# A long convolution and a mixture of experts on one core: eight batches in groups of 1, 2, 2, 2 and 1 in place of four groups of 2

## The chip, the core and the metric
The kernel runs on one core of a Trainium2 chip. The core has five engines with queues of their own: PE multiplies matrices and writes PSUM, DVE and ACT work on vectors in SBUF and PSUM, POOL (GpSimd) works on SBUF and issues the indirect transfers, SP issues nearly all others. The metric is the device time of one execution in microseconds (us), as a median of runs. Programs are compared on the same chip.

## The reference
There are 8 batches of 5696 tokens with 128 channels. First comes a causal convolution over the sequence with one filter `h` for each channel, done through a Fourier transform of twice the length. Its result is the input of a mixture of 8 experts: each token takes the one with the highest logit.
```python
y = irfft(rfft(x, n=2*S, axis=1) * rfft(h, n=2*S, axis=0)[None], n=2*S, axis=1)[:, :S]
x = y.reshape(B * S, D)                       # 45568 tokens of 128
logits = x @ w_gate + modality_bias[modality_id]
e_idx = argmax(logits, axis=1); probs = softmax(logits); gate_w = probs[range(N), e_idx]
for e in range(8):
    mask = e_idx == e
    out[mask] = gate_w[mask, None] * (maximum(x[mask] @ w1[e], 0) @ w2[e])   # 128 -> 1024 -> 128
```

## The kernel before
Most products are made from fp32 data split in two parts of a shorter type (`high`, `low`): ACT casts the high part, DVE or POOL subtracts it for the low part, and three matmuls stand for one.

The Fourier transform is split into stages, with results in DRAM between them. Stage 1 (`stage1`, for the first group `stage1_first`) transforms along 64 rows for each of 45 values of `q` and stores `z`. Stages 2 and 3 (`stage23`) go over 64 values of `k`: a matmul (`over`, L637), the product with the filter on DVE (L644), additions on POOL or DVE (L650, L651), the split of the sum into `yh` (ACT, L654) and `yl` (DVE or POOL, L657), the matmuls back (L663, or L667 to L669) and a store of `u`. Stage 4 (`stage4`) loads `u`, transforms back to tokens (L755, L756 or L761), turns them (L773), makes the logits (L780) and, by chunks of up to 4 pairs of `q`, routes: which expert, which place in the table `rows`, and an indirect store of 128 rows each by POOL (L880). A group is 2 batches; there are four, and they go through the stages one after the other, with the next group's earlier stages beside the later ones of this.

After some chunks (`CUTS`) the rows known so far are cut into a level of tiles of 512 rows of one expert; a table (`level`) says which expert and which rows. There are 7, 7, 22, 22 and 23 full tiles (0 to 80), and 23 tiles of 256 for what is left. A tile (`experts`) loads its rows (`mrt`, L962), turns them (L984), splits them, and goes through 8 steps of `gemm1` (L998 to L1000), `hh` (ACT, L1003), `hl` (DVE, L1006) and `gemm2` (L1014 to L1016); then it is turned back (L1023), scaled (L1026) and scattered to `out` by POOL (L1030). Weights are needed split. In the first two levels (`RAW`) each tile loads them raw in four halves and splits them (L973 to L980); meanwhile `split_weights` writes split weights of all experts to DRAM, and later levels load those (L969) where the expert changes.

The order on every engine is made when the program is built: `Plan.run` takes steps with given costs and due times (`AIMS`: knots for each stage, a lead for each kind of step) and lists them as they would start; a step that DVE or POOL (or ACT) may do goes to the one that is free. The engines then run their lists strictly in order. `BURST` and `SPACE` keep POOL's indirect transfers apart.

Of the kernel before, what the change touches and what calls it, by code (L numbers as in the profile page):

```python
# [1224 lines left out]
```

## Time and profile before
| what | us |
|---|---|
| median of 3 runs (2198.26 to 2200.70) | 2199.54 |
| the profiled execution | 2207.35 |
| its span, first to last instruction | 2205.6 |
| PE busy | 2049.7 |
| DVE busy | 1509.3 |
| ACT busy | 1190.1 |
| POOL busy | 1294.9 |

Busy times are of the whole span; the granted clock was 0.963 on average. Matmuls are pipelined, so that a busy PE may still run below its rate: how far apart matmuls start says more than how long one is recorded. A wait is put down to the instruction whose signal came last.

### The profile page before, as it was taken

The numbers are of one execution on the slowest core, as the hardware profiler recorded it, in microseconds if no ns is written. First come the engines' busy times: TensorE is split into PE (matmuls) and PEld (weight loads), VectorE is DVE, ScalarE is ACT, GpSimd is POOL, SyncE is SP. The second block draws the span as 40 slices with busy tenths as digits, with TensorE's granted clock in tenths as the row PEclk, the third lists the DMA queues.
The fourth block names the chain that finished last, engine by engine and source line by source line (L and its number), as shares of the span: only waits on it lengthen the run. The fifth ranks groups of instructions, "written<-read, shape, count | busy, mean of one in ns | idle before, by whom it ended". The sixth has DMA issues, their size and how long they took to land. (4 is left out here: it accounts for less than half of the span.)

```text
span 2205.6 us, 38243 instructions
## 1 busy us (share of the span) xinstructions
PE 2049.7 (93%) x11222; PEld 1677.4 (76%) x11222; DVE 1509.3 (68%) x2901; ACT 1190.1 (54%) x2415; POOL 1294.9 (59%) x1676
## 2 busy tenths in 40 slices
PE   5699989989999679999999999999999899999997
PEld 5577867767777567778887778888887688888997
DVE  5468936778557778977765899867677455555554
ACT  5645645445555456557764445566664344444443
POOL 2155726567577777745777777557777634334333
PEclk8889999999999989999999999999999999999999
DMA  8999899998998679965654656644341621214520
GB/s 276 312 297 319 278 280 319 309 281 270 315 307 252 200 216 287 280 210 161 202 182 146 199 156 185 204 157 125 120 150 58 148 68 44 84 42 159 191 75 21
DMA packets 236497, 434.77 MB, mean 197 GB/s; under 512 B 37317, under 2 KB 103849, under 8 KB 231680
## 3 DMA queue, kind: packets, MB, share of 16 engines
q1 hardware_dynamic: 212608, 384.17, 55.8%
q0 software_dynamic: 23680, 48.15, 6.7%
q8 instruction: 90, 1.47, 0.3%
q14 instruction: 119, 0.97, 0.1%
HBM read 408.13 MB, written 176.22 MB: 265 GB/s over the span
## 5 line engine op out<-in xcount | busy, mean ns | idle before, releaser
L1006 DVE SCALAR_TENSOR_TENSOR hl<-bank,hh 128x512 fp32r<-128x512 f32 x740 | 502.9, 686 | 264.2 <-ACT hh L1003 259.1
L1003 ACT ACTIVATE hh<-bank 128x512 fp32r<-128x512 f32 x740 | 440.1, 598 | 389.0 <-PE bank L1000 350.0
L1030 POOL DMA_INDIRECT out<-of,mrt x370 | 371.5, 1004 | 370.5 <-DVE of L1026 257.4
L880 POOL DMA_INDIRECT rows<-rt,idx x360 | 365.5, 1015 | 175.4 <-issue 102.3
L644 DVE TENSOR_TENSOR t<-bank,hs 96x512 f32<-96x512 f32 x420 | 266.9, 677 | 57.4 <-PE bank L637 29.7
L1014 PE MATMUL bank<-hh,slot 128*128 128x512 f32 (+1 forms) x736 | 304.1, 413 | 1.5 <-ACT hh L1003 1.2
L998 PE MATMUL bank<-mxh,slot 128*128 128x512 f32 (+1 forms) x736 | 302.6, 411 | 2.9 <-DVE hl L1006 1.0
L1015 PE MATMUL bank<-hl,slot 128*128 128x512 f32 (+1 forms) x736 | 283.2, 385 | 6.6 <-DVE hl L1006 6.6
L999 PE MATMUL bank<-mxl,slot 128*128 128x512 f32 (+1 forms) x736 | 284.6, 387 | 0.3
L1000 PE MATMUL bank<-mxh,slot 128*128 128x512 f32 (+1 forms) x736 | 283.9, 386 | 0.0
L1016 PE MATMUL bank<-hh,slot 128*128 128x512 f32 (+1 forms) x736 | 283.1, 385 | 0.0
L637 PE MATMUL bank<-zb,m 96*96 96x256 f32 x896 | 235.7, 391 | 12.6 <-DMA zb<-z 4.6
L637 PEld LDWEIGHTS bank<-zb,m 96*96 96x96 f32 x896 | 145.4, 167 | 61.5 <-DVE t L644 6.6
L654 ACT CAST yh<-t 96x512 fp32r<-96x512 f32 x142 | 87.4, 619 | 148.3 <-POOL t L651 60.0
L998 PEld LDWEIGHTS bank<-mxh,slot 128*128 128x128 f32 x736 | 141.6, 192 | 34.0 <-issue 3.0
L1000 PEld LDWEIGHTS bank<-mxh,slot 128*128 128x128 f32 x736 | 141.1, 192 | 29.5
L1016 PEld LDWEIGHTS bank<-hh,slot 128*128 128x128 f32 x736 | 140.2, 190 | 29.0
L1015 PEld LDWEIGHTS bank<-hl,slot 128*128 128x128 f32 x736 | 141.3, 192 | 27.2 <-DVE hl L1006 7.4
L458 ACT COPY ut<-bank 90x512 f32<-90x512 f32 x206 | 117.8, 580 | 81.8 <-PE bank L663 39.9
L1014 PEld LDWEIGHTS bank<-hh,slot 128*128 128x128 f32 x736 | 141.2, 192 | 26.6 <-issue 3.8
L999 PEld LDWEIGHTS bank<-mxl,slot 128*128 128x128 f32 x736 | 141.9, 193 | 23.7 <-DVE mxl L990 1.3
L657 POOL TENSOR_TENSOR yl<-t,yh 96x512 fp32r<-96x512 f32 x88 | 115.3, 1316 | 69.8 <-ACT yh L654 63.0
(232 smaller groups left out, 4075.8 us busy)
## 6 DMA issues: line engine op xcount, KB each, us to landing
slot<-weights SPq DMA_DIRECT2D x156, 1024.0 KB
z<-z SPq DMA_DIRECT2D x180, 256.0 KB
uu<-u SPq DMA_DIRECT2D x159, 256.0 KB
zb<-z SPq DMA_DIRECT2D x112, 360.0 KB
u<-ut SPq DMA_DIRECT2D x112, 360.0 KB
raw<-in_w SPq DMA_DIRECT2D x88, 256.0 KB
mrt<-rows SPq DMA_DIRECT2D x81, 260.0 KB
hs<-hd SPq DMA_DIRECT2D x96, 192.0 KB
```

The lines of the kernel that those rows point to most:

```text
L637: nc.tensor.matmul(two(st["px"])[:KP, h], mm, both["zb"][:, k % 2, 1 - h], start=True, stop=True)
L644: nc.vector.tensor_tensor(st[f"t{h}"].rearrange("p j (b d) -> p j b d", d=D), px[:KP, h].rearrange("p (b d) -> p b d", d=D).unsqueeze(1).t ...
L880: nc.gpsimd.indirect_dma_start(views[count[0] % NVIEW], bass.IndirectOffsetOnAxis(ap=rs["idx"][:, t + c:t + c + 1], axis=0), st["rt"][:, c ...
L998: nc.tensor.matmul(po, w[0][:, fs], xh, start=True, stop=False)
L999: nc.tensor.matmul(po, w[0][:, fs], xl, start=False, stop=False)
L1000: nc.tensor.matmul(po, w[1][:, fs], xh, start=False, stop=True)
L1003: nc.scalar.activation(hf["hh"], hf["ph"], AF.Relu)
L1006: nc.vector.scalar_tensor_tensor(hf["hl"], hf["ph"], 0.0, hf["hh"].bitcast(F32), op0=ALU.max, op1=ALU.subtract)
L1014: nc.tensor.matmul(po, w[0][:, fs], hf["hh"][:, cs], start=k == 0, stop=False)
L1015: nc.tensor.matmul(po, w[0][:, fs], hf["hl"][:, cs], start=False, stop=False)
L1016: nc.tensor.matmul(po, w[1][:, fs], hf["hh"][:, cs], start=False, stop=k == 7)
L1030: nc.gpsimd.indirect_dma_start(oviews[(t * NSUB + c) % NVIEW], bass.IndirectOffsetOnAxis(ap=st["rt"].bitcast(I32)[:, c, D + 1:D + 2], axis=0),
```

## The change
- The groups are 1, 2, 2, 2, 1 batches. A group of one takes two values of `k` together in `over`, `product` and `drain`, so that a matmul keeps its 256 columns there; in stages 1 and 4 its matmuls have 128. The filter is transformed with the first batch: one tile of 256 columns, one tensor `z`, no `zh` and no tile `hz`.
- `stage1_first` works on 1, 2, 3, 4 and then 5 values of `q` at a time with one load and one split for all of them, and stores `z` by pairs. The arithmetic of the router's bias moved behind it.
- The cuts are after (group 0, last chunk), (1, fifth), (1, last), (2, last), (3, last): levels of 3, 15, 7, 22, 22, 12 and 23 tiles. The first four levels split raw weights (47 tiles, not 14), from one buffer `whole` of 1 MB that is loaded only where the expert changes.
- The last level goes over three pairs of weight buffers, not four. The logits of two pairs of `q` are made together.
- The planner's costs are other numbers, and all due times (`AIMS`).
```diff
-NG = 4
-GB = B // NG
+GROUPS = (1, 2, 2, 2, 1)
+NG = len(GROUPS)
+FIRST = [sum(GROUPS[:g]) for g in range(NG)]
+GB = max(GROUPS)
 GC = GB * D
-GW = (GC + D,) + (GC,) * (NG - 1)
+GW = ((GROUPS[0] + 1) * D,) + tuple(n * D for n in GROUPS[1:])
 TSL = 256
 QF = 5
+QS = (1, 2, 3, 4) + (QF,) * 7
...
-    "tiles": (-720, -305, 173, 709, 65, 220, 453),
+    "tiles": (40, 231, 596, 804, 967, -130, 4458, 4389),
...
-CUTS = [(0, 4), (0, 6), (1, 6), (2, 6)]
-RAW = 2
+CUTS = [(0, 6), (1, 4), (1, 6), (2, 6), (3, 6)]
+RAW = 4
...
-RUNS = (1,) * RAW + (2,) * (len(LEVELS) - 1 - RAW) + (4,)
+RUNS = (1,) * RAW + (2,) * (len(LEVELS) - 1 - RAW) + (3,)
...
-    SYNC = {"PE": 1.89, "DVE": 0.149, "ACT": 0.149, "POOL": 0.219, "SP": 0.1, "-": 0.0}
-    LAND = 3.41
-    RATE = 0.3000e6
+    SYNC = {"PE": 1.166, "DVE": 0.114, "ACT": 0.102, "POOL": 0.505, "SP": 0.1, "-": 0.0}
+    LAND = 3.95
+    RATE = 0.2866e6
     ROWS = 58e3
     BURST = 4, 7.13, 4.97
     SPACE = 4, 0.85
+    TURN = 200
...
-        for q in range(NQ):
-            ...
-            z = sp.tile([128, 2, GC], F32, name="z0", bufs=4)
-            zf = sp.tile([128, 2, D], F32, name="zf", bufs=4)
-            nc.scalar.copy(z, ps[:, :, :GC])
-            nc.vector.tensor_copy(zf, ps[:, :, GC:w])
-            for dst, src in ((zd[0], z), (zh, zf)):
-                nc.sync.dma_start(dst[2 * q:2 * q + 2].rearrange("e k t c -> (e k) (t c)"), src.rearrange("p t c -> p (t c)"))
+        for n in QS:
+            ft = sp.tile([128, QF, 2, 4, 64], F32R, name="ft0")
+            fs = sp.tile([128, QF, 2, 64], F32, name="fs")
+            xt = sp.tile([128, QF, w], F32, name="xt0", bufs=3)
+            xx = sp.tile([128, 2, QF, w], F32R, name="xx0")
+            nc.sync.dma_start(fs[:, :n].rearrange("p q i k -> p q (i k)"), fq[:, q0:q0 + n])
+            nc.sync.dma_start(xt[:, :n], xq[0][:, q0:q0 + n])
+            fv = ft.bitcast(F32)
+            nc.scalar.copy(ft[:, :n, 0, 1:3, :], fs[:, :n])
+            nc.gpsimd.tensor_tensor(ft[:, :n, 1, 1:3, :], fs[:, :n], fv[:, :n, 0, 1:3, :], op=ALU.subtract)
+            nc.scalar.copy(xx[:, 0, :n], xt[:, :n])
+            nc.vector.tensor_tensor(xx[:, 1, :n], xt[:, :n], xx.bitcast(F32)[:, 0, :n], op=ALU.subtract)
+            nc.scalar.activation(ft[:, :n, :, 0, :], fv[:, :n, :, 2, :], AF.Copy, scale=sgn[:, 0:1])
+            nc.scalar.activation(ft[:, :n, :, 3, :], fv[:, :n, :, 1, :], AF.Copy, scale=sgn[:, 0:1])
+            for j in range(n):
+                q = q0 + j
+                ps = ps1.tile([128, 2, w], F32, name="ps")
+                for t in range(2):
+                    for m, (a, b) in enumerate(((0, 0), (1, 0), (0, 1))):
+                        nc.tensor.matmul(ps[:, t], ft[:, j, a, 2 * t:2 * t + 2, :], xx[:, b, j], start=m == 0, stop=m == 2)
+                if q % 2 == 0:
+                    z = sp.tile([128, 2, 2, w], F32, name="z0", bufs=3)
+                if q % 2:
+                    nc.scalar.copy(z[:, 1], ps)
+                else:
+                    nc.vector.tensor_copy(z[:, 0], ps)
+                if q % 2 or q == NQ - 1:
+                    m = q % 2 + 1
+                    nc.sync.dma_start(zd[0][2 * (q + 1 - m):2 * q + 2].rearrange("(a e) k t c -> (e k) a (t c)", a=m),
+                                      z[:, :m].rearrange("p a t c -> p a (t c)"))
...
-        if lv >= RAW:
-            nc.vector.tensor_tensor(tmp_[:, 1:], ev_[:, 1:], ev_[:, :nt - 1], op=ALU.not_equal)
-            for i in range(0, nt, -(-nt // RUNS[lv])):
-                nc.vector.memset(tmp_[:, i:i + 1], 1.0)
-            nc.vector.tensor_copy(tab[:, 2 * nt:], tmp_)
+        nc.vector.tensor_tensor(tmp_[:, 1:], ev_[:, 1:], ev_[:, :nt - 1], op=ALU.not_equal)
+        for i in range(0, nt, -(-nt // RUNS[lv])):
+            nc.vector.memset(tmp_[:, i:i + 1], 1.0)
+        nc.vector.tensor_copy(tab[:, 2 * nt:], tmp_)
...
+    whole_w = wp.tile([128, 2, FF], F32, name="whole")
...
-        wpair[:] = ws + [spare[:2], spare[2:]]
+        wpair[:] = ws + [spare[:2]]
...
+            def over(_, st=st, zs=zs, odd=odd):
+                zv = zs["zb"][:, :, :, :gb * D] if g == 0 else rows_of(zs["zb"])[:, odd * ks:(odd + 1) * ks]
                 for h, mm in ((0, m2), (1, m1)):
-                    nc.tensor.matmul(two(st["px"])[:KP, h], mm, both["zb"][:, k % 2, 1 - h], start=True, stop=True)
+                    po = two(st["px"])[:KP, h]
+                    if ks == 1:
+                        nc.tensor.matmul(po, mm, zv[:, 0, 1 - h], start=True, stop=True)
+                    else:
+                        nc.tensor.matmul(po.rearrange("p (k c) -> p k c", k=ks), mm, zv[:, :, 1 - h], start=True, stop=True)
...
-                    prev = step({"POOL": 1.35}, dispatch, [ga, tk, prev], due + 6 + 0.2 * c,
+                    prev = step({"POOL": 1.55}, dispatch, [ga, tk, prev], due + 6 + 0.2 * c,
...
+                if len(some) == 2 or pi == len(chunk) - 1:
+                    lg = step({"PE": 0.07 * sum(x[2] for x in some)}, partial(logits, some=some), [*turns, *logit_steps[-1:]], due + 4,
+                              () if logit_steps else ((score_sl, "pa"),), st=rs)
+                    logit_steps.append(lg)
...
-            def load_raw(_, i, half, hs, lv=lv, j=j, n_lv=n_lv):
+            def load_raw(_, lv=lv, j=j, n_lv=n_lv):
                 tab = tabs[lv][0]
                 ex = nc.sync.value_load(tab[0:1, n_lv + j:n_lv + j + 1], min_val=0, max_val=E - 1)
-                nc.sync.dma_start(half["raw"], w12_d[bass.ds(ex, 1), :, i, hs].rearrange("o p f -> (o p) f"))
-
-            def w_high(_, i, half, hs, sn=sn):
-                nc.scalar.copy(wpair[sn][i][:, 0, hs], half["raw"])
-
-            def w_low(e, i, half, hs, sn=sn):
-                engine[e].tensor_tensor(wpair[sn][i][:, 1, hs], half["raw"], wpair[sn][i].bitcast(F32)[:, 0, hs], op=ALU.subtract)
+                ch = nc.sync.value_load(tab[0:1, 2 * n_lv + j:2 * n_lv + j + 1], min_val=0, max_val=1)
+                nc.sync.dma_start(whole_w, w12_d[bass.ds(ex, 1)].rearrange("o p i f -> (o p) i f"), cond=ch > 0)
+
+            def w_high(_, i, hs, sn=sn):
+                nc.scalar.copy(wpair[sn][i][:, 0, hs], whole_w[:, i, hs])
+
+            def w_low(e, i, hs, sn=sn):
+                engine[e].tensor_tensor(wpair[sn][i][:, 1, hs], whole_w[:, i, hs], wpair[sn][i].bitcast(F32)[:, 0, hs], op=ALU.subtract)
...
+            if lv < RAW:
+                at = d0 - d
+                lw = step({"SP": 1.6}, load_raw, [*tw, *split], at - 0.4 * d, nbytes=1.05e6 * min(1, (E + 1) / n_lv), order=lw)
+                split = []
+                for i in range(2):
+                    lows = []
+                    for k in range(2):
+                        how = dict(i=i, hs=slice(k * (FF // 2), (k + 1) * (FF // 2)))
+                        hi = step({"ACT": 0.54}, partial(w_high, **how), [lw, users.get((sn, i))], at + (0.2 * i + 0.1 * k) * d)
+                        lows.append(step({"DVE": 0.62, "POOL": 1.27}, partial(w_low, **how), [hi], at + (0.2 * i + 0.1 * k + 0.05) * d))
+                    ww.append(lows)
+                    split += lows
...
-                prev = step({"POOL": 1.35}, partial(scatter, c=c), [prev], d0 + d * (2 + c / ns),
+                prev = step({"POOL": 1.5}, partial(scatter, c=c), [prev], d0 + d * (2 + c / ns),
```
Three places in the order. First SP's list in the first stage: loads `xt` of one `q` and stores `z`, `zh` before.
```order
L369 DMA xt_248<-in_xq 128x384
L379 DMA z<-z_181 128x512
L379 DMA zh<-zf 128x256
L369 DMA xt_266<-in_xq 128x384
L379 DMA zh<-zf 128x256
L369 DMA xt_342<-in_xq 128x384
L379 DMA zh<-zf 128x256
L369 DMA xt_367<-in_xq 128x384
```
The same stage on SP now, a few loads in.
```order
L363 DMA fs<-in_fq 128x640
L364 DMA xt_350<-in_xq 128x1280
L363 DMA fs<-in_fq 128x640
L364 DMA xt_407<-in_xq 128x1280
L386 DMA z<-z_157 128x2x512
L386 DMA z<-z_232 128x2x512
L386 DMA z<-z_262 128x2x512
```
A load is of five `q` of 256 columns where it was one of 384, and the stores of `zh` are gone.

Second DVE's list at the 21st tile (`hl` is the tile's own step), before:
```order
L1006 SCALAR_TENSOR_TENSOR hl_2608<-bank_1047,hh_2604 128x512
L1006 SCALAR_TENSOR_TENSOR hl_2606<-bank_1049,hh_2602 128x512
L768 COPY rt_1088<-tokid 128x4
L734 TENSOR_TENSOR gt<-gs_1077,gt 128x2x128
L747 TENSOR_TENSOR uu_1081<-uu_1081 128x512 x2
L1006 SCALAR_TENSOR_TENSOR hl_2609<-bank_1051,hh_2605 128x512
L1026 TENSOR_TENSOR of_2612<-bank_1052,mrt_2597 128x512
```
DVE at the same tile now; `slot` is a half of the split weights:
```order
L678 TENSOR_TENSOR t_738<-t_740,t_738 96x256
L679 TENSOR_TENSOR t_738<-t_738,t_740 96x256
L1024 TENSOR_TENSOR slot_1729<-whole,slot_1729 128x512 x2
L1050 SCALAR_TENSOR_TENSOR hl_1745<-bank_722,hh_1741 128x512
L1024 TENSOR_TENSOR slot_1730<-whole,slot_1730 128x512
L1050 SCALAR_TENSOR_TENSOR hl_1746<-bank_717,hh_1742 128x512
L1024 TENSOR_TENSOR slot_1730<-whole,slot_1730 128x512
L1070 TENSOR_TENSOR of_1749<-bank_718,mrt_1734 128x512
L685 TENSOR_TENSOR yl_744<-t_738,yh_742 96x512
```
The four halves of the tile's weights and the additions and `yl` of another group's stage 3 stand between the `hl` of this tile.

Third POOL's list at the end of the second group's routing (`rows`: indirect stores; `rows<-padt`: a store that waits for them; `out`: scatters of a tile), before:
```order
L880 DMA rows<-rt_1092,idx_1096 369152x130 x2
L534 TENSOR_TENSOR spread<-spread 128x36 x3
L880 DMA rows<-rt_1092,idx_1096 369152x130 x2
L1083 DMA rows<-padt 512x1x130
L1030 DMA out<-of_2612,mrt_2597 45568x128 x4
L534 TENSOR_TENSOR spread<-spread 128x36 x3
L1030 DMA out<-of_2611,mrt_2594 45568x128 x4
L657 TENSOR_TENSOR yl_1075<-t_1072,yh_1073 96x512
L650 TENSOR_TENSOR t_1068<-t_1071,t_1068 96x256
```
POOL at its first cut of that group now:
```order
L922 DMA rows<-rt_757,idx_764 369152x130
L543 TENSOR_TENSOR spread<-spread 128x36 x3
L922 DMA rows<-rt_758,idx_764 369152x130 x4
L543 TENSOR_TENSOR spread<-spread 128x36 x3
L922 DMA rows<-rt_761,idx_764 369152x130 x4
L1128 DMA rows<-padt 512x1x130
L678 TENSOR_TENSOR t_738<-t_741,t_738 96x256
L679 TENSOR_TENSOR t_738<-t_738,t_741 96x256
L685 TENSOR_TENSOR yl_745<-t_738,yh_743 96x512
```
A long run of transfers, 35 before and 37 now, still stands ahead of the next additions and `yl`.

## Rows read from the trace of the kernel before
**Rows 1.** The page's head: span, then busy us of each engine.
```profile
span 2205.6 us, 38243 instructions
...
PE 2049.7 (93%) x11222; PEld 1677.4 (76%) x11222; DVE 1509.3 (68%) x2901; ACT 1190.1 (54%) x2415; POOL 1294.9 (59%) x1676
```
**Rows 2.** Stretches: length, each engine's busy us, granted clock, DMA share, GB/s.
```profile
0.00:105.00 105.00, 68.68 (x270) 59.04 (x270) 59.02 (x104) 65.11 (x119) 21.98 (x51) 0.85 0.90 301
165.00:275.00 110.00, 108.26 (x615) 89.01 (x614) 101.58 (x155) 69.07 (x140) 75.54 (x77) 1.00 0.92 299
486.00:1471.00 985.00, 923.29 (x5025) 745.90 (x5023) 754.81 (x1468) 565.56 (x1179) 683.93 (x821) 0.97 0.71 221
715.00:830.00 115.00, 83.53 (x406) 66.57 (x405) 88.84 (x177) 55.57 (x115) 86.19 (x96) 0.88 0.69 206
990.00:1471.00 481.00, 469.45 (x2661) 385.00 (x2659) 373.15 (x711) 285.85 (x581) 333.72 (x404) 0.98 0.58 180
1705.00:1760.00 55.00, 44.40 (x193) 35.00 (x192) 26.61 (x62) 20.04 (x34) 35.20 (x52) 0.91 0.58 135
2035.00:2206.00 171.00, 153.27 (x1223) 148.57 (x1222) 84.28 (x143) 72.49 (x142) 61.56 (x92) 0.95 0.29 95
```
**Rows 3.** Line L984: ns min/median/max, first and last start in us.
```profile
L984 PE MATMUL bank<-ident,mrt x370: 270/272/472, 486.3 to 2178.8; 128*128 128x128 f32 x185
```
**Rows 4.** Timeline of PE, the 161st of L984: start us, us, instruction.
```profile
1471.04 0.63 PE L984 MATMUL bank<-ident,mrt 128*128 128x128 f32 x4
```
**Rows 5.** Who PE waits for, 715 to 830: total us, times, longest.
```profile
PE bank L669 <- POOL yl L657: 18.9, 1, 18.9
PE bank L1015 <- DVE hl L1006: 6.3, 1, 6.3
```
**Rows 6.** Timeline of POOL, 764 to 783 us.
```profile
780.48 0.98 POOL L1030 DMA_INDIRECT out<-of,mrt  x1 [0.30 <-issue]
781.48 1.28 POOL L657 TENSOR_TENSOR yl<-t,yh 96x512 fp32r<-96x512 f32 x1
```
**Rows 7.** Who PE waits for, 1705 to 1760 us.
```profile
PE bank L984 <- DMA mrt<-rows: 9.9, 2, 7.7
```
**Rows 8.** DMA issues: out<-in, queue, count, KB of one.
```profile
xt<-in_xq SPq DMA_DIRECT2D x45, 192.0 KB
...
zh<-zf SPq DMA_DIRECT2D x45, 128.0 KB
```
**Rows 9.** Timeline of PE at 1800 us.
```profile
1799.73 0.39 PE L999 MATMUL bank<-mxl,slot 128*128 128x512 f32 x1
1799.96 0.40 PE L1000 MATMUL bank<-mxh,slot 128*128 128x512 f32 x1
```
**Rows 10.** Groups of DVE by form: count, busy us, mean ns, idle before.
```profile
L644 DVE TENSOR_TENSOR t<-bank,hs 96x512 f32<-96x512 f32 x420 | 266.9, 677 | 57.4 <-PE bank L637 29.7 <-DMA hs<-hd 9.8 <-POOL t L651 4.6
L650 DVE TENSOR_TENSOR t<-t,t 96x256 f32<-96x256 f32 x110 | 63.3, 575 | 0.7
...
L747 DVE TENSOR_TENSOR uu<-uu 128x512 fp32r<-128x512 f32 x67 | 49.7, 762 | 1.2 <-ACT uu L743 0.8
L657 DVE TENSOR_TENSOR yl<-t,yh 96x512 fp32r<-96x512 f32 x54 | 47.0, 872 | 36.4 <-ACT yh L654 36.1
L980 DVE TENSOR_TENSOR slot<-raw,slot 128x512 fp32r<-128x512 f32 x43 | 30.8, 716 | 27.2 <-ACT slot L977 27.0
...
L734 DVE TENSOR_TENSOR gt<-gs,gt 128x256 fp32r<-128x256 f32 x44 | 20.5, 466 | 12.1 <-ACT gt L731 12.1
```
**Rows 11.** Timeline of DVE, 757 to 786 us.
```profile
756.77 0.41 DVE L650 TENSOR_TENSOR t<-t,t 96x256 f32<-96x256 f32 x1
...
758.64 0.67 DVE L657 TENSOR_TENSOR yl<-t,yh 96x512 fp32r<-96x512 f32 x1
...
784.80 1.24 DVE L657 TENSOR_TENSOR yl<-t,yh 96x512 fp32r<-96x512 f32 x1 [19.44 <-ACT yh L654]
```

More of the change, by code (lines that the diff above doesn't have):

```diff
@@ L202, in first @@
             nonlocal woken
-            apart = begun[-self.BURST[0]] + self.BURST[1 if now < AIMS["tiles"][0] else 2]
+            apart = begun[-self.BURST[0]] + self.BURST[1 if now < self.TURN else 2]
             kept = now >= apart and any(r[2].lag for r in ready["POOL"])
@@ L560, in stage1 @@
             ld = step({"SP": 0.9}, load, after if i == 0 else (), due - 9, ((ft_sl, "ft"), (xt_sl, "xt")), st=st,
-                      nbytes=400e3, early=EARLY, order=last)
+                      nbytes=(0.66e5 + 0.67e5 * gb) * n, early=EARLY, order=last)
             last = ld
-            sg = step({"ACT": 0.82}, signs, [ld], due - 2, st=st)
+            sg = step({"ACT": 0.62}, signs, [ld], due - 2, st=st)
             for j in range(n):
@@ L591, in stage23, with rows_of, load @@
         use = early if g == 0 else usual
-        t_sl, yh_sl, yl_sl, zb_sl, ut_sl, hs_sl, filt_sl = (use[x] for x in ("t", "yh", "yl", "zb", "ut", "hs", "hz"))
+        t_sl, yh_sl, yl_sl, zb_sl, ut_sl, hs_sl = (use[x] for x in ("t", "yh", "yl", "zb", "ut", "hs"))
         ft = {}
         whole = WHOLE_ROWS[g]
-        for k in range(K1):
-            due = along(knots, k / K1)
+        gb = GROUPS[g]
+        ks = GB // gb
+        def rows_of(t):
+            return t.rearrange("p a i c -> p (a i c)").rearrange("p (k i c) -> p k i c", i=2, c=gb * D)
+        kl = KH if g == 0 else 2 * ks
+        for k in range(0, K1, ks):
+            due = along(knots, k / K1)
+            odd = k // ks % 2
+            if k % kl == 0:
+                zs = {"left": []}
+                def load(_, zs=zs, k=k):
+                    nc.sync.dma_start(zs["zb"][:90].rearrange("p k i c -> p (k i c)"),
+                                      zd[g][:, k:k + kl].rearrange("e k i c -> e (k i c)"))
+                lz = step({"SP": 0.45}, load, after if k == 0 else (), due - 10, ((zb_sl, "zb"),), st=zs, nbytes=368e3, early=EARLY,
+                          order=lz)
             if k % KH == 0:
@@ L684, in stage23 @@
-            hi = None if whole else step({"ACT": 0.62}, high, [ad], due + 3, ((yh_sl, "yh"),), st=st)
-            lo = ad if whole else step({"DVE": 0.84, "POOL": 1.34}, low, [hi], due + 4, ((yl_sl, "yl"),), ((t_sl, "t1"),), st=st)
+            ad = step({"POOL": 1.5, "DVE": 0.82}, add, [pr], due + 2, free=((t_sl, "t0"),), st=st)
+            hi = None if whole else step({"ACT": 0.55}, high, [ad], due + 3, ((yh_sl, "yh"),), st=st)
+            lo = ad if whole else step({"DVE": 0.68, "POOL": 1.28}, low, [hi], due + 4, ((yl_sl, "yl"),), ((t_sl, "t1"),), st=st)
@@ L712, in stage4 @@
             rs = {}
-            pairs, logit_steps = [], []
+            pairs, logit_steps, some, turns = [], [], [], []
             t0 = 0
@@ L782, in stage4 @@
                 us = tuple((uus, f"uu{j}") for j in range(n))
-                last = step({"SP": 1.35}, load, after if i == 0 else (), due - 9, ((gs_sl, "gs"), *us), st=st, nbytes=590e3, early=EARLY, order=last)
-                g1 = step({"ACT": 0.61 if whole else 0.41}, gt_high, [last], due - 4, ((gws if whole else gt_sl, "gt"),), st=st)
+                last = step({"SP": 1.35}, load, after if i == 0 else (), due - 9, ((gs_sl, "gs"), *us), st=st, nbytes=(0.66e5 + 1.31e5 * gb) * n, early=EARLY, order=last)
@@ L785, in stage4 @@
+                g1 = step({"ACT": 0.62 if whole else 0.33}, gt_high, [last], due - 4, ((gws if whole else gt_sl, "gt"),), st=st)
                 need = [g1]
                 if not whole:
-                    g2 = step({"DVE": 0.6}, gt_low, [g1], due - 3, free=((gs_sl, "gs"),), st=st)
-                    need = [step({"ACT": 0.82}, gt_turn, [g2], due - 2, st=st)]
+                    g2 = step({"DVE": 0.36}, gt_low, [g1], due - 3, free=((gs_sl, "gs"),), st=st)
+                    need = [step({"ACT": 0.64}, gt_turn, [g2], due - 2, st=st)]
@@ L789, in stage4 @@
                     for j in range(n):
-                        uh = step({"ACT": 0.62}, partial(uu_high, j=j), [last], due - 4 + j, st=st)
-                        need.append(step({"DVE": 0.74, "POOL": 1.32}, partial(uu_low, j=j), [uh], due - 3 + j, st=st))
-                lpy = step({"PE": (0.88 if whole else 0.71) * n}, back, [*need, lpy], due, ((banks, "py"), (rt_sl, "rt")),
+                        uh = step({"ACT": 0.1 + 0.215 * gb}, partial(uu_high, j=j), [last], due - 4 + j, st=st)
+                        need.append(step({"DVE": 0.08 + 0.27 * gb, "POOL": 0.15 + 0.56 * gb}, partial(uu_low, j=j), [uh], due - 3 + j, st=st))
@@ L916, in store @@
                     nc.sync.dma_start(ws_d[e, i, :, :, fs], pt["w"].bitcast(F32))
-                hi = step({"ACT": 0.4}, high, [ld], due + m, ((pre_sl, "w"),), st=pt)
-                got.append(step({"DVE": 0.65, "POOL": 0.82}, low, [hi], due + m + 1, st=pt))
+                hi = step({"ACT": 0.33}, high, [ld], due + m, ((pre_sl, "w"),), st=pt)
+                got.append(step({"DVE": 0.36, "POOL": 0.71}, low, [hi], due + m + 1, st=pt))
                 stores.append(step({"SP": 0.45}, store, [got[-1]], due + m + 3, free=((pre_sl, "w"),), st=pt, nbytes=262e3))
```

267 lines of the change are left out of this document (125 added, 142 removed), and 38 rows, old and new, of the table AIMS.

## The prediction
> **What bounds the kernel now.** I read the page's busy shares first, then the same by stretches, then who PE waits for, and last single instructions. PE is busy 2049.7 us of 2205.6, DVE 1509.3 [rows 1]: this is a PE kernel, but not in every stage, and a change that leaves the number of big matmuls alone can only win the time in which PE stands or runs slowly. The stretches show where that is [rows 2]. In the first 105 us PE has work for 68.7 us, and the DMA engines are 0.90 busy at 301 GB/s: that stage is bound by transfers. Expert tile 0 starts at 486.3 us, tile 40 at 1471.0 us [rows 3, 4]; between them PE is busy 923 of 985 us, DVE 755. Half of the idle time there lies in one place, 715 to 830 us, where PE is busy only 83.5 of 115 us at a granted clock of 0.88 (a mix of the levels 1.2 and 2.4 GHz: after each standstill records stretch). Two waits make it: 18.9 us for `yl` by POOL and 6.3 us for `hl` by DVE [rows 5]. The long one is an order that didn't fit: POOL's `yl` ran at 781.48, behind a row of scatters that each took 0.98 us with 0.30 us between [rows 6]. From 990 to 1471 us PE is busy 469.5 of 481 us, and after that nearly always, but for 1705 to 1760 us (44.4 of 55), where the rows of the last full tiles aren't there: 9.9 us [rows 2, 7]. So I split the time at tile 0 and at tile 40 and price the three parts.
>
> **Part one, to tile 0: 486 us become 480 (457 to 503).** The first group has one batch and the filter in place of two. Each of 45 loads shrinks from 192 to 128 KB, and the 45 separate stores of `zf`, 128 KB each, are gone [rows 8]: 45 x 192 KB = 8.85 MB less, at 301 GB/s 29 us. If all of it comes through, tile 0 starts at 457. Against it stands the queue: counted from the order of SP with the shapes of its rows, 137.0 MB were issued ahead of the row load of tile 0, now 142.2 MB, since parts of the next groups (and their own filter tables) are put ahead of it. 5.2 MB at 301 GB/s are 17 us: tile 0 at 503. Work on PE ahead of it is 9 us less (the stationary and moving sizes of the order, at the spacing of starts below). Neither end is nearer by the rows: the DMA engines are 0.90 busy here, so a tenth could take up more. I take the middle, 480. The bias arithmetic that moved behind this stage runs on DVE while PE and the queue go on; were that cover gone, it is inside the 46 us between the ends.
>
> **Part two, tile 0 to tile 40: 985 us become 968 (946 to 1034).** PE's matmuls of 512 columns start 0.23 us apart [rows 9]. With such spacings for every shape, the order has 878 us of PE work between the two tiles before and 898 now, since one more group passes through: 923 + 20 = 943 us busy. DVE gets much more. Counted from the order between the same two tiles, by the mean of its row [rows 10]: 89 more halves of raw weights (40 become 129, as four levels split on the fly and not two) x 0.716 = 64; 88 more half additions x 0.575 = 51; 70 more `yl` (51 become 121, POOL's fall from 77 to 30) x 0.872 = 61; 30 more `uu` x 0.762 = 23; 18 more products x 0.677 = 12; 15 more `gt` x 0.466 = 7; less 27 copies that go to ACT, at about the length of a product, 18. Sum 200: DVE needs 955 us where it needed 755. That is as much as PE. Those means hold waiting, though: a `yl` took 0.67 us at 758.64 and 1.24 us at 784.80, a half addition 0.41 us at 756.77 [rows 11]; at these undisturbed times (0.68 for raw halves and `uu`) the same counts add 164: 919 us. So DVE needs 919 to 955, PE 943. ACT gets 103 more casts of raw halves; at the length of a product they are 70 us on 566 of 985 in this stretch, and it hides them.
> What the rows show of the two lengths of `yl`: the short one ran while POOL issued transfers, the long one while POOL ran additions. The Trainium skill (SBUF — State Buffer, Who interferes with whom) says that a DVE instruction with two inputs in SBUF and a GpSimd instruction that reads SBUF shut each other out for their whole length. That speaks against this change, for nearly all it gives to DVE is of that kind; by it, with POOL as busy as before, the sum would go by 955, and with POOL's `yl` cut to 30 nearer to 919.
> I take 937, the middle, for DVE, so PE still leads by a hair, and give it the slack that PE had where nothing stood in its way, 481 over 469.5: 943 x 1.0245 = 966, and 2 for the places where DVE leads (by counts DVE is ahead of PE in tiles 10 to 25). That supposes that the two waits of 25 us go. The low end is PE's 943 with 3; the high end is DVE's 955 at the fullest that DVE was seen over 100 us, 101.6 of 110 [rows 2]: 1034.
>
> **Part three, tile 40 to the end: 735 us become 722.** The wait for the last full tiles: before, 75 us of PE work lay between the last transposed rows and tile 58, the first that needs all rows, and that was 8 to 10 us short [rows 7]. Now the last group is one batch, 12 full tiles hang on it, and the order has 118 us of PE work in between. I take the 10.6 us of idle time and 0.09 x 44 = 4 us of clock: -14. The tiles of 256 tokens rotate over three pairs of weight buffers and no longer four, so the second of them needs the pair that the last full tile used: 2.1 MB after its end, at 301 GB/s 7 us, beside a tile that takes 153.3 / 23 = 6.7 us of PE [rows 2]. Between 0 and 7 us; I take 4. PE work -2. 735 - 14 + 4 - 2 = 723, rounded with the rest to 722.
>
> **Sum.** 480 + 968 + 722 = 2170 us against a span of 2205.6, 35.6 less. The profiled execution itself took 2207.35, the median of the runs shown is 2199.54, 0.35% lower; I take the difference from the median: 2164 us.
>
> **Rivals.**
> *DVE becomes the bound.* Place: tiles 0 to 40. For it: its work rises by a quarter while PE's rises by 2%, and it feeds PE with `hl` on every one of 320 steps there. Against it: from 165 to 275 us both were above 0.92 at once. It decides from where DVE can't be filled over 95% (then the stretch passes 1004 us, which is 480 + 1004 + 722 = 2206). Full price: 503 + 1034 + 722 = 2259, 53 over the span: 2253 us.
> *The burst stays.* The wait for POOL isn't removed but moved. For it: POOL's order still has runs of 37 and 39 transfers ahead of additions that PE's chain needs (35 before `yl` until now). Against it: the planner now counts 1.55 and 1.5 us for one transfer where it counted 1.35, and the rows say 1.28 with gaps besides, so it no longer expects POOL too early. Price: the 31.5 us that PE lacks between 715 and 830 us: 2164 + 31 = 2195 us, about no change.
> *The early start holds.* The 29 us come through, and the stretch is PE's bare work. For it: the first stage was bound by transfers; against it the 142.2 MB. 457 + 946 + 718 (no wait for the third pair) = 2121, 85 under the span: 2115 us.
>
> **How the numbers follow.** Forecast 0.42, around 2164, its own range 2140 to 2190; the early start holds 0.20; the burst stays 0.12; DVE becomes the bound 0.26. A measurement of this kernel can't tell 0.2% (4.4 us) from no change. Faster: 0.40 of the forecast, 0.20, and 0.05 of the burst, 0.65. Same: 0.02 and 0.05, 0.07. Slower: 0.26 and 0.02, 0.28. For 8 in 10 I leave out the last few us of the early start and the upper half of DVE's case: 2112 to 2232.
>
> **What would show it.** Part one: the first stage over some 29 us earlier, and the first transposition of `mrt` between 457 and 503 us. Part two: DVE busy 919 to 955 us between tiles 0 and 40 (the 1st and the 161st transposition of `mrt`), and no wait of PE above 6 us that ends on POOL. Part three: no wait on `mrt` at tile 69, and one of 0 to 7 us on weights near the first tiles of 256. The forecast is wrong if PE's waits in part two end mostly on DVE and sum to over 60 us, or if tile 0 starts after 503 us.

## The result, and the profile after

The changed kernel takes 2174.09 us (median of 4 runs, 2171.78 to 2176.02), the kernel before 2200.12 beside it; the ratio is 0.9882, interval 0.9865 to 0.9899, 26 us less. The forecast was 2164, its own range 2140 to 2190. The profiled execution took 2175.41 us, its span is 2173.2. The spans of the two profiles are 32 us apart and not 26, for the profiled execution of before took some 7 us more than the median; the parts below are read from these two profiles.

The page's head of the changed kernel, busy us of each engine, to be laid beside [rows 1]:

```profile
PE 2052.7 (94%) x11707; PEld 1694.0 (78%) x11707; DVE 1623.6 (75%) x3285; ACT 1307.0 (60%) x2774; POOL 1266.6 (58%) x1603
```

PE kept its work, POOL has 28 us less, DVE 114 and ACT 117 us more. Its stretches (length, busy us of PE, PEld, DVE, ACT, POOL, granted clock, DMA share, GB/s), beside [rows 2]:

```profile
0.00:80.00 80.00, 47.16 (x273) 43.90 (x274) 44.34 (x48) 46.75 (x72) 25.04 (x51) 0.83 0.84 300
80.00:250.00 170.00, 148.70 (x786) 115.39 (x785) 88.63 (x174) 92.24 (x214) 64.85 (x82) 0.95 0.93 295
250.00:490.00 240.00, 221.15 (x1092) 166.67 (x1091) 151.31 (x333) 107.39 (x260) 118.54 (x169) 0.96 0.97 310
490.40:1457.40 967.00, 933.55 (x5524) 770.25 (x5524) 900.57 (x1831) 678.51 (x1464) 708.70 (x797) 0.98 0.71 219
1700.00:1760.00 60.00, 60.00 (x341) 47.80 (x341) 38.77 (x96) 34.52 (x85) 34.91 (x52) 1.00 0.25 76
```

The first stage of the kernel before, line L353 (first and last start in us behind the durations):

```profile
L353 PE MATMUL ps<-xx,ft x270: 332/339/689, 8.3 to 102.5; 128*128 128x384 f32 x135
```

Lines L377 (first stage) and L1028 (transposition of `mrt`) of the changed kernel:

```profile
L377 PE MATMUL ps<-xx,ft x270: 274/284/584, 5.0 to 71.5; 128*128 128x256 f32 x135
...
L1028 PE MATMUL bank<-ident,mrt x370: 270/273/475, 490.4 to 2151.0; 128*128 128x128 f32 x185
```

And the 161st of L1028 in PE's timeline, where tile 40 begins:

```profile
1457.43 0.66 PE L1028 MATMUL bank<-ident,mrt 128*128 128x128 f32 x4
```

So the three parts are 490.4, 967.0 and 715.8 us, where the forecast had 480, 968 and 722 and the kernel before 486.3, 984.7 and 734.6 [rows 3, 4]. The first stage ends at 71.5 us and no longer at 102.5, as forecast, but nothing of that is left at tile 0. Tiles 0 to 40 won 18 us, the end 19.

Who PE waits for between tiles 0 and 40 (us, times, longest), beside [rows 5]:

```profile
PE bank L874 <- DVE oh L869: 5.4, 3, 2.4
PE bank L1042 <- DVE hl L1050: 4.6, 2, 2.3
PE bank L697 <- DVE yl L685: 4.4, 3, 2.1
...
PE bank L697 <- POOL yl L685: 2.9, 2, 2.4
```

And from tile 40 to the end, the only line there, beside [rows 7]:

```profile
PE bank L1067 <- ACT ot L465: 0.8, 2, 0.5
```

The wait of 18.9 us for POOL and the one for the last rows are gone; what is left are waits of at most 3.2 us; in the whole list 25 of 36 us are for DVE. DVE's groups between tiles 0 and 40 (count, busy us, mean ns, idle before), beside [rows 10]:

```profile
L1024 DVE TENSOR_TENSOR slot<-whole,slot 128x512 fp32r<-128x512 f32 x126 | 100.7, 825 | 4.0 <-ACT slot L1021 3.8
L685 DVE TENSOR_TENSOR yl<-t,yh 96x512 fp32r<-96x512 f32 x120 | 92.2, 770 | 16.5 <-ACT yh L682 15.5 <-PE bank L696 0.6
L679 DVE TENSOR_TENSOR t<-t,t 96x256 f32<-96x256 f32 x112 | 50.6, 452 | 0.0
```

One moment on DVE's timeline (start us, us), beside [rows 11]:

```profile
977.56 4.22 DVE L1024 TENSOR_TENSOR slot<-whole,slot 128x512 fp32r<-128x512 f32 x1
```

And POOL's timeline at the same moment:

```profile
977.34 0.72 POOL L678 TENSOR_TENSOR t<-t,t 96x256 f32<-96x256 f32 x1
978.02 0.73 POOL L679 TENSOR_TENSOR t<-t,t 96x256 f32<-96x256 f32 x1
978.72 1.28 POOL L1024 TENSOR_TENSOR slot<-whole,slot 128x512 fp32r<-128x512 f32 x1
979.97 1.26 POOL L782 TENSOR_TENSOR uu<-uu 128x512 fp32r<-128x512 f32 x1
```

A raw half has a median of 681 ns on DVE; this one took 4.22 us, while POOL ran four two-input instructions back to back, and it ended 0.55 us after the last of them, little less than its median. Read the mean (825) against the median: the difference is standing, not work. The rest of the stretch agrees. Of the 542 instructions that DVE ran there on the five lines it shares with POOL (L678, L679, L685, L782, L1024), the 160 that overlap a `TENSOR_TENSOR` of POOL took 0.25 us over their undisturbed lengths (0.68 or 0.41 us) on average; the other 382 took no more than these, though 351 of them ran beside POOL's transfers. `hl`, which has one input in PSUM, took 0.68 us with a `TENSOR_TENSOR` of POOL beside it and without.

### The profile page after: what moved, and what is told of

Read it like the earlier page. It is cut to its first block, busy times and chain, and to the rows that moved or that the text cites. A ratio compares the mean times of both kernels' runs of the same rounds, so it can differ in the third digit from the quotient of the medians.

```text
span 2173.2 us, 39577 instructions
## 1 busy us (share of the span) xinstructions
PE 2052.7 (94%) x11707; PEld 1694.0 (78%) x11707; DVE 1623.6 (75%) x3285; ACT 1307.0 (60%) x2774; POOL 1266.6 (58%) x1603
## 5 line engine op out<-in xcount | busy, mean ns | idle before, releaser
L1074 POOL DMA_INDIRECT out<-of,mrt x370 | 382.6, 1034 | 355.0 <-DVE of L1070 238.7
L922 POOL DMA_INDIRECT rows<-rt,idx x360 | 391.4, 1087 | 176.3 <-issue 102.1
L1058 PE MATMUL bank<-hh,slot 128*128 128x512 f32 (+1 forms) x768 | 309.7, 403 | 0.0
L1042 PE MATMUL bank<-mxh,slot 128*128 128x512 f32 (+1 forms) x768 | 304.5, 396 | 4.7 <-DVE hl L1050 4.6
L1044 PE MATMUL bank<-mxh,slot 128*128 128x512 f32 (+1 forms) x768 | 290.3, 378 | 0.0
L1060 PE MATMUL bank<-hh,slot 128*128 128x512 f32 (+1 forms) x768 | 290.3, 378 | 0.0
L669 DVE TENSOR_TENSOR t<-bank,hs 96x512 f32<-96x512 f32 x384 | 242.1, 677 | 59.3 <-PE bank L659 47.8
L659 PE MATMUL bank<-zb,m 96*96 96x256 f32 x768 | 201.5, 391 | 12.0 <-ACT z L465 3.6
L582 PE MATMUL bank<-xt,ft 128*128 128x256 f32 (+1 forms) x720 | 164.3, 367 | 16.0 <-DMA ft<-in_fq 6.9
L659 PEld LDWEIGHTS bank<-zb,m 96*96 96x96 f32 x768 | 124.3, 168 | 55.1 <-ACT z L465 9.4
L1060 PEld LDWEIGHTS bank<-hh,slot 128*128 128x128 f32 x768 | 144.8, 189 | 28.7
L1058 PEld LDWEIGHTS bank<-hh,slot 128*128 128x128 f32 x768 | 145.4, 189 | 22.8 <-issue 2.0
L582 PEld LDWEIGHTS bank<-xt,ft 128*128 128x128 f32 x720 | 127.5, 196 | 38.8 <-ACT ft L572 12.2
```

The lines of the kernel that those rows point to most:

```text
L582: nc.tensor.matmul(two(zt["ps"])[:, t, :gc], st["ft"][:, j, 2 * t:2 * t + 2, :], narrow(st["xt"], gc)[:, j], start=True, stop=True)
L659: nc.tensor.matmul(po, mm, zv[:, 0, 1 - h], start=True, stop=True)
L922: nc.gpsimd.indirect_dma_start(views[count[0] % NVIEW], bass.IndirectOffsetOnAxis(ap=rs["idx"][:, t + c:t + c + 1], axis=0), st["rt"][:, c ...
L1042: nc.tensor.matmul(po, w[0][:, fs], xh, start=True, stop=False)
L1044: nc.tensor.matmul(po, w[1][:, fs], xh, start=False, stop=True)
L1058: nc.tensor.matmul(po, w[0][:, fs], hf["hh"][:, cs], start=k == 0, stop=False)
```

## The experiments

They ran on chips where the kernel before took 2209 to 2212 us and the changed kernel wasn't run again, so ratios to the kernel before are compared, and 0.9882 stands for the changed kernel: a ratio higher by 0.0010 is 2.2 us. Each ratio carries about 0.002 either way, so a difference under some 6 us says nothing. The stretches are of single profiles, not scaled for the chip; these put tile 0 between 487 and 496 us where nothing ahead of it was touched (the changed kernel, e3, e5, e6).

**Four doses of work beside PE.** The subtraction that makes the low part of a raw half, and the cast that makes the high part:

```diff
 def w_low(e, i, hs, sn=sn):
+    for _ in range(1 if hs.start else 2):      # e1; e2: range(2); e3: only if t < 2
     engine[e].tensor_tensor(wpair[sn][i][:, 1, hs], whole_w[:, i, hs], ...)
 def w_high(_, i, hs, sn=sn):
+    for _ in range(2):                         # e4 alone
     nc.scalar.copy(wpair[sn][i][:, 0, hs], whole_w[:, i, hs])
```

> The subtraction that makes the low part of a raw weight half is issued twice for the first half of each row of weights, in the order of the changed kernel: 63 more on DVE between tiles 0 and 40, at 0.68 to 0.83 us 43 to 52 us more of DVE work, which goes from 900 to about 947 us of 967. Theory (PE leads, DVE has 67 us of room): the time rises by 0 to 15 us, to 2174-2189. Rival (DVE already sets the pace there): it rises by 43 to 52 us, to 2217-2226.

> The same subtraction issued twice for every half: 126 more on DVE between tiles 0 and 40, 86 to 104 us, so that DVE would need 986 to 1004 us where the stretch takes 967. Theory (PE leads with 67 us of room on DVE): the room is used up and the rest shows, 35 to 90 us more, 2209-2264, and PE's waits in the stretch now end on DVE. Rival (DVE already sets the pace): the whole 86 to 104 us, twice what the half dose costs, 2260-2278.

> The same subtraction is left out from tile 2 on, so the low parts of the raw weights are stale there: DVE loses 118 of 126 instructions between tiles 0 and 40, 80 to 97 us. Theory (PE leads): PE's matmuls remain, only the waits on DVE of that stretch can go (19 us of PE's idle time ended on DVE), so 5 to 20 us faster, 2154-2169. Rival (DVE sets the pace): all 34 us that PE stands idle between tiles 0 and 40 go, 30 us or more faster, 2144 or less.

> The cast that makes the high part of a raw weight half is issued twice: 126 more on ACT between tiles 0 and 40, at 0.60 us 75 us, which goes from 678 to 753 us of 967. Theory (ACT hides the casts, as forecast): within 5 us of the changed kernel, 2170-2179. Rival (the casts stand in the chain from the weights' arrival to the matmul, and ahead of hh in ACT's queue): 10 to 75 us slower, 2184-2249.

Measured: 0.9987 [0.9970, 1.0003], 1.0264 [1.0244, 1.0285], 0.9676 [0.9652, 0.9699] and 0.9887 [0.9867, 0.9907], which is +23, +84, -45 and +1 us against the changed kernel. Tiles 0 to 40 of e1 (columns as in the stretches above):

```profile
497.60:1486.10 988.50, 942.49 (x5524) 772.10 (x5524) 950.44 (x1890) 678.35 (x1464) 725.43 (x813) 0.98 0.70 214
```

The same of e2:

```profile
503.40:1540.50 1037.10, 955.35 (x5525) 772.11 (x5525) 997.48 (x1954) 676.37 (x1464) 757.36 (x827) 0.98 0.67 204
```

Of e3:

```profile
494.90:1418.80 923.90, 914.05 (x5524) 761.98 (x5524) 807.97 (x1707) 678.91 (x1464) 626.14 (x771) 1.00 0.75 229
```

And of e4:

```profile
494.90:1459.70 964.80, 935.98 (x5524) 765.01 (x5523) 881.04 (x1830) 761.59 (x1616) 689.21 (x798) 0.99 0.72 220
```

ACT hides its casts: 83 us more of them cost nothing, as the theory of e4 said. DVE doesn't hide its halves: 50 us more of DVE cost 23, 97 us more cost 84, 93 us less give 45. No one theory holds through: e1 lies between its two, e2 in the range of "PE leads" and just under the rival's, e3 in the rival's. PE and DVE share the bound. Tiles 0 to 40 alone became 22 and 70 us longer and 43 us shorter: near the changed kernel's load a microsecond of DVE is worth about half of one, and the second 47 us of e2 cost 49 there. The rest of e2's 84 lies ahead of tile 0 (503.4 us) and behind tile 40, where raw halves are split too.

PE's waits for DVE in the stretch, summed over the whole list, are 25 us in the changed kernel, 43 in e1, 75 in e2 and 9 in e3. The relief of e3 is more than all of the 25: for the same 5524 matmuls PE is busy 914 and not 934 us at a granted clock of 1.00 and not 0.98 (a mean between the levels of 1.2 and 2.4 GHz). So the standstills that went gave 24 us of idle time and 19 us of busy time; the ratio of the clocks (0.985 and 0.998) makes some 13 of the 19, an estimate. The dose isn't DVE's alone: POOL makes some of the halves, and its busy time in the stretch changes by +17, +49 and -83 us. How far that matters is not told apart here.

**Relief for DVE by other ways.** e5: tiles 18 to 46 load weights that are already split, at a change of expert; e6: the gate of tiles 0 to 39 on ACT.

```diff
-nc.scalar.copy(wpair[sn][i][:, 0, hs], whole_w[:, i, hs])               # e5, levels 2 and 3; w_low goes
+nc.sync.dma_start(wpair[sn][i].bitcast(F32), ws_d[bass.ds(ex, 1), i]..., cond=ch > 0)
-nc.vector.tensor_tensor(st["of"][:, :ns], blocks(st["pq"])[:, :ns], ...)  # e6, tiles 0 to 39
+for c in range(ns):
+    nc.scalar.activation(st["of"][:, c], blocks(st["pq"])[:, c], AF.Copy, scale=st["rt"][:, c, D:D + 1])
```

> Tiles 18 to 46 (levels 2 and 3) no longer split raw weights: they load weights already split, once per change of expert in each of two runs of tiles, at the place in the order where the cast stood. 116 casts and 116 subtractions fewer (about 90 of them on DVE between tiles 18 and 40, some 62 to 74 us), against some 20 MB more to load over 400 us, in which the DMA engines were busy 0.56 to 0.69. Theory after the first four runs (DVE and PE share the bound, a microsecond of DVE is worth half a microsecond of time): in the run that left the low halves out, tiles 18 to 40 were 13 us shorter, so about 13 us less than the changed kernel, ratio to before 0.980 to 0.985. Rival (PE leads, the room is there): 0 to 4 us, ratio 0.986 to 0.990. Rival (the loads wait for the buffers at the head of SP's queue and hold up others): slower than the changed kernel, ratio over 0.990.

> The multiplication by the gate of tiles 0 to 39 goes from DVE (38 instructions of 0.68 us between tiles 0 and 40, 26 us) to ACT (four instructions for each of them, since its factor is one number per row; unknown by the trace, 0.3 to 0.6 us each, 46 to 91 us on 678 of 967). Theory (DVE and PE share the bound, half a microsecond per microsecond of DVE): about 13 us less than the changed kernel, ratio to before 0.980 to 0.985. Rival (only the sum of raw halves matters, or ACT's hh is held up by the new work): no gain or slower, ratio 0.988 or more.

Measured: 0.9882 [0.9859, 0.9905] and 0.9895 [0.9872, 0.9917], no gain in either, as a rival of each had it. The profile of e5 is of the fastest of its four executions (2173.5 us, the median is 2184.7). Its tiles 0 to 40:

```profile
487.40:1455.60 968.20, 931.59 (x5524) 766.64 (x5524) 839.66 (x1754) 631.43 (x1372) 663.57 (x790) 0.99 0.75 230
```

The two longest entries of PE's waits in that stretch of e5:

```profile
PE bank L1052 <- DMA slot<-weights: 4.0, 1, 4.0
PE bank L875 <- DVE oh L872: 3.6, 2, 2.7
```

Tiles 0 to 40 of e6:

```profile
496.10:1472.70 976.60, 939.69 (x5525) 770.89 (x5525) 881.00 (x1794) 710.19 (x1616) 704.80 (x799) 0.98 0.71 217
```

And PE's longest entry there:

```profile
PE bank L695 <- ACT yh L682: 6.8, 4, 4.3
```

In e5 DVE is 61 us lighter and the stretch is as long. PE's longest wait is now for weights, and of the 43 us that tiles 0 to 40 lost in e3, 23 lay in tiles 7 to 18 (the starts of their first transpositions: 261.5 us became 238.3), which e5 doesn't touch. But tiles 18 to 40, which it does relieve, gained nothing either: 478.7 us, for 474.2 in the changed kernel and 460.6 in e3. In e6 DVE loses 20 us and ACT gets 32 in four short instructions for each tile, and PE's wait for ACT's `yh` goes from 3.3 to 6.8 us. Half a microsecond per microsecond of DVE is no price list. That the 20 MB of weights (e5) and ACT's new work (e6) ate the gain fits these waits, but no run shows it alone.

**Transfers ahead of tile 0.** 

```diff
 nc.sync.dma_start(xt[:, :n], xq[0][:, q0:q0 + n])          # e7: issued twice
 nc.sync.dma_start(narrow(st["xt"], gc)[:, :n], xq[g][:, q0:q0 + n])
+if g == 1:
+    nc.sync.dma_start(narrow(st["xt"], gc)[:, :1], xq[g][:, q0:q0 + 1])        # e8: into the same buffer
+    nc.sync.dma_start(whole_w[:, ..., ...][:, :n * gc], xq[g][:, q0:q0 + n])   # e9: into one that is free
```

> Each load of the first stage's data is issued twice, 5.9 MB more in the first 70 us. Theory (transfers bound the way to tile 0, as forecast): at 290 to 300 GB/s the first stage ends 20 us later and tile 0 starts 20 us later (510 us), and the whole is 15 to 20 us longer, ratio to before 0.995 to 0.998. Rival (the stage before tile 0 has room later on, where the queue catches up): the first stage is later, tile 0 and the whole by 0 to 8 us, ratio 0.988 to 0.992.

> One of each two loads of data of the second group is issued twice, 5.9 MB more between about 75 and 400 us. Theory (the queue of transfers ahead of tile 0 sets its start, whichever they are): tile 0 20 us later (510 us), ratio to before 0.995 to 0.998, like the extra loads of the first stage. Rival (what the first group waits for sets tile 0, transfers of the next group lie beside it): tile 0 and the whole by 0 to 8 us, ratio 0.988 to 0.992.

> The second group's data is loaded a second time, now into a buffer that nothing else uses before tile 0, so that no load waits for an earlier one: 5.9 MB more between about 75 and 400 us and no new wait. (The run before this, with the repeated load into the same buffer, moved 3.0 MB more, and 23 loads waited 86.5 us at the head of SP's queue.) Theory (transfers bound the way to tile 0, whichever they are): 5.9 MB at 290 to 310 GB/s, tile 0 some 20 us later (510 us), ratio to before 0.994 to 0.998. Rival (only what the first group's chain waits for counts; in the run before it was the wait at the head of SP's queue): tile 0 and the whole by 0 to 8 us, ratio 0.988 to 0.992.

Measured: 0.9949 [0.9930, 0.9967], 1.0151 [1.0124, 1.0178], 0.9937 [0.9914, 0.9960]. The expectation of e8 had its bytes wrong: 23 loads of 128 KB are 3.0 MB. First and last start of the transposition of `mrt` in e7:

```profile
L1029 PE MATMUL bank<-ident,mrt x370: 270/272/421, 512.5 to 2178.9; 128*128 128x128 f32 x185
```

In e8:

```profile
L1030 PE MATMUL bank<-ident,mrt x370: 270/272/330, 556.8 to 2219.8; 128*128 128x128 f32 x185
```

SP's own waits in e8 between 70 and 460 us, the longest entry:

```profile
SPq L569 <- DMA xt<-in_xq: 86.5, 23, 6.8
```

The transposition in e9:

```profile
L1031 PE MATMUL bank<-ident,mrt x370: 270/272/363, 506.1 to 2175.0; 128*128 128x128 f32 x185
```

And the stretch from 80 to 250 us of e9:

```profile
80.00:250.00 170.00, 143.92 (x713) 110.77 (x712) 79.68 (x130) 86.38 (x188) 55.61 (x69) 0.93 0.95 307
```

5.9 MB more cost 22 and 16 us at tile 0 (against 490.4) and 15 and 12 us in the end, whether they belong to the first group (e7) or to the second (e9); 5.9 MB at 300 GB/s are 20. The whole time lies just under the range of the theory in both (0.995 and 0.994) and over the rival's 0.992, which e9's interval still touches. Two things speak for the theory. In e9 none of the added loads waited for an earlier one, where in e7 SP stood 9.5 us for that; and by the traces 148.8 MB had moved up to tile 0 in the changed kernel, 154.4 in e7 and 154.6 in e9, at 303, 301 and 306 GB/s. So it is the amount of all transfers ahead of tile 0 that sets its start. e8, outside both ranges of its expectation, shows another thing: a load into a buffer that an earlier load still fills waits at the head of SP's queue with everything behind it. The rate up to tile 0 falls to 272 GB/s, and half the bytes cost 59 us, four to five times as much.

**POOL's share given to DVE.**

```diff
-engine[e].tensor_tensor(...)     # add, yl, uu, low part of raw halves
+nc.vector.tensor_tensor(...)
```

> Every half addition and subtraction that POOL shared with DVE is given to DVE, in the order of the changed kernel: between tiles 0 and 40 POOL loses some 185 us of work, DVE gets 79 halves of 0.68 us and 91 smaller ones of 0.41 us, 91 us by their undisturbed lengths. Theory (two-input instructions of DVE stand while POOL reads the same memory: 74 us of DVE's 900 are lengths above the undisturbed ones): most of these 74 go, DVE is busy 920 to 950 us, and the time changes by 0 to +25 us, ratio to before 0.988 to 0.999. Rival (POOL's share is a pure relief for DVE): DVE needs 985 us or more and the time rises as in the run with the doubled subtraction, by 60 us or more, ratio 1.015 or more.

Measured: 2165.87 us, 0.9798 [0.9764, 0.9831]: faster than the changed kernel, whose interval begins at 0.9865, by some 18 us, and outside both ranges of the expectation. Tiles 0 to 40 of e10:

```profile
491.70:1446.20 954.50, 928.78 (x5525) 759.37 (x5524) 901.20 (x1988) 675.18 (x1466) 542.96 (x641) 1.00 0.73 222
```

Its line L1024 on DVE over the span (ns min/median/max; in the changed kernel 659/681/4218 for 154):

```profile
L1024 DVE TENSOR_TENSOR slot<-whole,slot x188: 659/680/780, 467.4 to 1529.0; 128x512 fp32r<-128x512 f32 x188
```

And three groups of DVE from 490 to 1457 us (`hl` and two that POOL had shared):

```profile
L1050 DVE SCALAR_TENSOR_TENSOR hl<-bank,hh 128x512 fp32r<-128x512 f32 x318 | 212.5, 680 | 19.7 <-ACT hh L1047 15.0 <-issue 4.1
L685 DVE TENSOR_TENSOR yl<-t,yh 96x512 fp32r<-96x512 f32 x156 | 106.2, 683 | 7.7 <-issue 3.6 <-PE bank L1044 1.4 <-ACT yh L682 1.1
L678 DVE TENSOR_TENSOR t<-t,t 96x256 f32<-96x256 f32 x151 | 62.6, 414 | 0.1
```

DVE ran 157 instructions more in 901.2 us busy; without them it had needed 900.6 in the changed kernel, and 881.0 to 901.4 in e4 and e7 to e9, which have the same DVE instructions. By undisturbed lengths the 157 are over 80 us, and they cost DVE 0 to 20: of what POOL took off DVE's hands, DVE had lost three quarters or more again by standing. The longest raw half fell from 4218 to 780 ns, the mean of `yl` from 770 to 683; `hl` has 680 in both. So the mechanism is that of the theory, and it went further than the 920 to 950 us that it gave DVE. The Trainium skill (SBUF — State Buffer, Who interferes with whom) says that a DVE instruction with two SBUF inputs and a GpSimd instruction that reads SBUF exclude each other; the runs agree, and show the price in this kernel. Why the time fell, with DVE as busy as before, is not shown in full: PE's waits for DVE went from 25 to 15 us in the stretch, and the granted clock from 0.98 to 1.00. That POOL, 166 us lighter, also issued its transfers sooner may be part of the gain; PE had waited only 2.9 us on POOL.

**Two pieces of the change put into the kernel before.**

```diff
-prev = step({"POOL": 1.35}, dispatch, ...)           # e11; scatter: 1.35 to 1.5
+prev = step({"POOL": 1.55}, dispatch, ...)
-CUTS = [(0, 4), (0, 6), (1, 6), (2, 6)]              # e12
+CUTS = [(0, 4), (0, 6), (1, 6), (2, 6), (3, 4)]
-    "tiles": (-720, -305, 173, 709, 65, 220, 453),           # and a due time for the new level
+    "tiles": (-720, -305, 173, 709, 65, 172.8, 220, 453),
```

> The kernel before, with one part of the change alone: the planner counts 1.55 and 1.5 us for a transfer issued by POOL where it counted 1.35. Theory (the planner expected POOL too early, which put a row of scatters ahead of the addition that PE waited 18.9 us for): no wait of PE on POOL above 6 us between tiles 0 and 40, and that stretch some 20 to 35 us shorter, ratio to before 0.984 to 0.992. Rival (the wait was an accident of one order, and a new order has others): the wait on POOL goes, other waits take its place, ratio 0.995 to 1.010.

> The kernel before, with the last full tiles divided: 16 of the 23 hang on the rows up to the fifth part of the last group, and only 7 on the last rows. Theory (the 9.9 us that PE stood at tile 58 were the wait for the last rows, because all 23 tiles hung on them): no wait of PE on mrt at tile 58, and 10 to 16 us less from tile 40 to the end (735 to 719-725 us), ratio to before 0.992 to 0.996. Rival (the table of one more level on DVE and its fence cost as much, or the same wait comes at the new division): 730 us or more from tile 40 to the end, ratio 0.997 or more.

Measured: 1.0096 [1.0061, 1.0130] and 1.0026 [1.0007, 1.0045]; both rivals. PE's waits between tiles 0 and 40 of e11, the longest entries:

```profile
PE bank L637 <- DMA zb<-z: 9.5, 3, 3.9
PE bank L669 <- POOL yl L657: 6.5, 1, 6.5
PE bank L1015 <- DVE hl L1006: 6.3, 2, 5.6
PE bank L669 <- DVE yl L657: 5.7, 3, 2.6
PE bank L569 <- ACT ft L559: 5.6, 1, 5.6
```

PE's waits in e12 from 1700 to 1770 us:

```profile
PE bank L984 <- DMA mrt<-rows: 8.5, 4, 3.1
```

And SP's timeline of e12 there:

```profile
1738.10 8.08 SPq L1125 DMA_DIRECT2D rows<-padt  x6
1748.07 1.25 SPq L969 DMA_DIRECT2D slot<-weights  x2
1753.77 0.01 SPq L962 DMA_DIRECT2D mrt<-rows  x1
1754.25 1.89 SPq L1125 DMA_DIRECT2D rows<-padt  x2
```

In e11 the long wait on POOL shrinks from 18.9 to 6.5 us, but the new order has others, and tiles 0 to 40 take 1001.9 us (before 984.7). In e12 the wait for rows stays, in four pieces (tiles 55, 56, 58 and 59): at tile 58 it is 3.1 us for 7.7 before. SP issues the load of tile 58 at 1753.77 us (before: 1747.59), behind six of the eight pad rows that close the last group. Between 1700 and 1770 us SP no longer waits for stores of rows (before: 5.6 us), but 39.5 us and not 15.5 for scatters of earlier tiles, which free the buffers of `mrt`. From tile 40 to the end it takes 741.2 us. Not tried: logits one by one, the raw load at every tile.

## Why the prediction was right, and where it wasn't

**Part one (480, measured 490.4).** The step that failed is the middle between the ends: "a tenth could take up more". The 29 us of the first stage came (31), and the queue took all of them back and 4 more: what the engines took up was 2 to 3%, not a tenth. Ahead of tile 0 stand 142.2 MB; over 490.4 us that is 290 GB/s, before 137.0 MB over 486.3, 282. For 480 it would have had to be 296. (These are counts of what SP issues; by the traces 144.5 MB had moved before and 148.8 now, at 297 and 303 GB/s.) e7 and e9 show why: behind the first stage the engines are 0.93 to 0.97 busy, so each MB moved ahead of tile 0 costs about 3 us there. The term "what of the 29 us comes through" was sized at 6 and measured at -4, which by the spread of tile 0 is none.

**Part two (968, measured 967.0).** The sum hits, its reason only by half. Right: the two long waits went, no wait on POOL over 6 us is left, and PE's idle time fell from 62 to 33 us. The hit is two misses that cancel: PE is busy 934 us and not 943, and idle 33 and not 25. The first fits the clock, which the 943 had carried along from before (0.965 there, 0.985 now); how much of it is the clock isn't shown. DVE needed 900.6 us, under the forecast's 919 to 955. The counts held in the main (126 raw halves for 129, 120 `yl` for 121), but only 76 half additions came for the 88, and the lengths didn't hold. The term that missed most is those half additions, priced at 51 us, 36 undisturbed: all that DVE ran of them in the stretch took 90.4 us before and 99.2 now, 9 us more, since their mean fell from 611 to 443 ns. That of `yl` fell from 856 to 769. POOL was no less busy in all (709 us for 684), but its `TENSOR_TENSOR` work fell from 321 to 266 us, and that is what DVE stands beside. Even the low end had kept the standing that is in the 755 us of before. Wrong: "PE still leads by a hair", with DVE hidden. e1 to e3 show that the bound is shared, and most of PE's waits end on DVE. The factor 1.0245 that I took for the slack of a stretch without hindrance covered that by its size, not by its reason. The rival that DVE becomes the bound was real with 97 us more of it (e2: slower than the kernel before), not with the 146 that the change added.

**Why the burst went.** I had argued that the planner counts POOL's transfers longer. e11 says that this alone gains nothing. What removed the wait is the whole new order; which part of it stays open.

**Part three (722, measured 715.8).** The wait for the last rows is gone, tile 69 waits for nothing: up to the first tile of 256 the time fell by 14.9 us (565.1 to 550.2), where -14 and -2 were forecast. The third weight pair is the term that was mis-sized: it cost nothing, at the low end of 0 to 7, and the tiles of 256 took 165.5 us for 169.4 before, 4 us less where 4 more were forecast. That 12 tiles and not 23 hang on the last rows fits the first; e12 didn't isolate it, since there other waits came as the one for the last rows went.

**The sum.** 2170 was forecast for the span and 2173.2 measured, but the parts were off by +10, -1 and -6 us, so that part of the hit is luck. Of the 10 us between 2164 and 2174.09, 7 come from the last step: the span of before was 6 us over the median of its kernel, the changed kernel's is 1 us under it.
